# Two PSUM tiles per running sum, part of the layer norm on ScalarE, and sums of x behind the Relu, in an attention and gated MLP kernel

## Chip, cores and metric

The kernel runs on one core of a Trainium2 chip. The metric is the device time of one execution, in microseconds (us). The kernel before takes 684.58 us, the median of 3 runs (684.27 to 684.89). Its profiled execution took 684.64 us, and the span of its trace, from the first to the last instruction, is 682.9 us.

## The reference

Eight batches, 12 heads, 448 positions, 64 columns a head; d_model is 768, d_ff 1024. All data are float32.

```python
scores = scale * np.matmul(q, k.transpose(0, 1, 3, 2)) - np.log(S)
attn = 1.0 / (1.0 + np.exp(-scores))
x = np.matmul(attn, v)                      # then (B, S, 768)
h = np.maximum(x @ w_in, 0.0)
u, v = h[..., :512], h[..., 512:]
mu = np.mean(v, axis=-1, keepdims=True)
var = np.mean((v - mu) ** 2, axis=-1, keepdims=True)
v_n = (v - mu) / np.sqrt(var + 1e-06)
v_s = np.einsum('ts,bsd->btd', w_spatial, v_n) + b_spatial[None, :, None]
out = (u * v_s) @ w_out
```

So it is attention with a sigmoid, and a gated MLP whose gate is the normalised half of the hidden values, mixed over the positions.

## The kernel before

**Precision.** A float32 operand is split into a high part, rounded to the type that TensorE takes, and a low part, the remainder. A product is three matmuls: high by high, low by high, high by low (`TERMS`).

**Stages.** The loop over m = 0 to 3 takes two batches at a time, b0 = 2m and b1 = 2m + 1. Each m goes through:

1. attention: scores, sigmoid, products with the values; the result is x in two parts (`x_s`);
2. the gate stage: `gate_values` for the row tiles (0, 1), (2, 3), (4, 5) and (6,) of the 896 positions. TensorE makes the gate half of the hidden values into PSUM tile pv, 18 matmuls for a row tile and 36 for a pair. ScalarE takes the Relu into rv (L606). VectorE makes statistics (L610, L611), GpSimd the power -0.5 of the variance (L613, L614), VectorE subtracts the mean (L616, "centring"), multiplies by rstd into the high part (L628) and forms the low part (L629);
3. the spatial stage: `spatial` multiplies with w_spatial into four PSUM tiles pg, one for each batch and half of the columns; `spatial_shorts` does the eight short matmuls of the last 64 positions (L658) for all four tiles; `biased` adds the bias on VectorE (L700) and so frees a tile of pg;
4. the block stage, only for m > 0: `gated_by_blocks` makes the other half of the hidden values for both batches from seven products of blocks (a scheme with fewer products than eight). Each product is 18 matmuls, two halves of nine, one for each 128 columns. The seven add up in the PSUM tiles ua, uw and uz; between the products the running sums are copied out by ScalarE (L775) or added to sums in SBUF by VectorE (L778). `settle` applies Relu and gate, splits the result and leaves it for the output. For m = 0 `gated` does all products plainly;
5. the output: six products po of 24 matmuls, each copied out by ScalarE and stored.

The products of blocks need sums of parts of x (t2, t3, t4, t1). They are made on VectorE and ScalarE in small steps: `x_sums` is a generator of 21 steps, and `spare(n)` takes the next n of them. `gate_values` calls `spare` ahead of the Relu (8, 2, 3, 3 steps for the four groups) and once again (1 step) behind the centring. `spare(99)` behind the gate stage takes what is left. `x_last_sum` then makes t1 in place in `x_s`: three passes over 1344 columns on VectorE, a cast on ScalarE, and a last subtraction on VectorE (L582, L584, L122, L123).

**Order.** Nothing is scheduled: `in_program_order` ties each instruction to the one before on its engine, so an engine's order is that in which the code issues. Loads are issued on SP in the same way; `load_block` brings weight blocks (768 KB) into four slots as they come free.

**PSUM.** `banks(name)` takes the next of four tiles of two banks each, in turn. A tile with i = 0 and 1 holds both halves of a product, one per bank; a write to a tile waits for the readers of that tile. In the block stage `products(ps, pos, mv, begins, then)` runs the two halves, and behind each one `then(i)` copies it out or adds it.

Of the kernel before, what the change touches and what calls it, by code (L numbers as in the profile page):

```python
# [8 lines left out]
F32 = mybir.dt.float32  # L9
F32R = mybir.dt.float32r  # L10
U32 = mybir.dt.uint32
AF = mybir.ActivationFunctionType
ALU = mybir.AluOpType
# [22 lines left out]
def attn_gmlp_kernel(  # L36
# [393 lines left out]
    def spare(n):  # L430

        while jobs and n:
            if next(jobs[0], None):
                n -= 1
            else:
                jobs.pop(0)
# [150 lines left out]
    def gate_values(m, ts):  # L587

        n = len(ts)
        pv = banks(f"pv_{m}_{ts[0]}")  # L590
        for i, t in enumerate(ts):
            product(
                pv[:, i, :F],
                [
                    (
                        lambda a, cc=cc, t=t: x_s[:, a, cc, t * P : (t + 1) * P],
                        lambda c, cc=cc: w_g_s[:, cc, c, :],
                    )
                    for cc in range(NCC)
                ],  # L600
            )
        if n > 1:
            load_weights(1 if ts[0] else 5)
        spare({0: 8, 2: 2, 4: 3, 6: 3}[ts[0]])
        rv = work.tile([P, 2, 512], F32, tag="tmp", name=f"rv_{m}_{ts[0]}", bufs=3)
        nc.scalar.activation(rv[:, :n], pv[:, :n], AF.Relu)  # L606
        mv = work.tile([P, 2, 2], F32, tag="mv", name=f"mv_{m}_{ts[0]}")
        for i in range(n):
            stats = work.tile([P, 6], F32, tag="stats", name=f"stats_{m}_{ts[i]}")
            nc.vector.bn_stats(stats, rv[:, i])  # L610
            nc.vector.bn_aggr(mv[:, i], stats)  # L611
        rstd = work.tile([P, 2], F32, tag="rstd", name=f"rstd_{m}_{ts[0]}")
        nc.gpsimd.tensor_scalar_add(rstd[:, :n], mv[:, :n, 1], 1e-6)  # L613
        nc.gpsimd.tensor_tensor(rstd[:, :n], rstd[:, :n], mhalf[:, :n], op=ALU.pow)  # L614
        for i in range(n):
            nc.vector.tensor_scalar_sub(rv[:, i], rv[:, i], mv[:, i, 0:1])  # L616
        load_weights(n - 1)
        spare(1)
        for i, t in enumerate(ts):
            vn = slots["tile"][:, t]  # L620
            if t != NFULL:
                parts = [(vn[:, 0], vn[:, 1], slice(0, P))]
            else:

                a, c = slice(0, HALF), slice(HALF, P)
                parts = [(vn[a, 0], vn[c, 0], a), (vn[c, 1], vn[a, 1], c)]
            for hi, lo, rows in parts:
                nc.vector.tensor_scalar_mul(hi, rv[rows, i], rstd[rows, i : i + 1])  # L628
                nc.vector.scalar_tensor_tensor(  # L629
                    lo,  # L630
                    rv[rows, i],
                    rstd[rows, i : i + 1],
                    hi.bitcast(F32),
                    op0=ALU.mult,
                    op1=ALU.subtract,
                )
            vns[t] = vn
        if n == 1:
            load_weights(1)
# [84 lines left out]

    def settle(b, fcs, g, pu):

        nc.vector.scalar_tensor_tensor(g, pu, 0.0, g, op0=ALU.max, op1=ALU.mult)
        if b % 2:
            gs = [slots["tile"][:, fcs[0] + a, :, :S] for a in range(2)]
        elif b > 1 and not fcs[0]:  # L730
            gs = [slots["tile"][:, 4 + a, :, :S] for a in range(2)]
        else:
            gs = work.tile([P, 2, 2 * S], F32R, tag="split", name=f"gs_{b}_{fcs[0]}", bufs=3)
            gs = [gs[:, a].rearrange("p (i s) -> p i s", i=2) for a in range(2)]
        split(gs[0], gs[1], g, nc.scalar.copy)
        for i, fc in enumerate(fcs):
            hidden[b, fc] = [part[:, i] for part in gs]
        load_weights(2)

    def gated_by_blocks(m):  # L740

        b0, b1 = 2 * m, 2 * m + 1
        x = {
            name: [
                x_s[:, :, k * KH + ks, j * S : (j + 1) * S] for ks in range(KH)
            ]
            for name, k, j in (("11", 0, 0), ("21", 1, 0), ("22", 1, 1), ("t1", 0, 1))
        }
        x |= sums
        r1, r2 = (work.tile([P, 2, S], F32, tag="v", name=f"ur_{m}_{n}", bufs=2) for n in range(2))  # L750
        r3 = work.tile([P, 1024], F32, tag="raw", name=f"ur_{m}_2", bufs=4)[:, : 2 * S].rearrange(
            "p (i s) -> p i s", i=2
        )

        def products(ps, pos, mv, begins, then=None):
            w = block(pos)
            ops = [(a, ks, c) for ks in range(KH) for a, c in TERMS]
            for i in range(2):
                for n, (a, ks, c) in enumerate(ops):
                    col = (ks * 2 + i) * P  # L760
                    nc.tensor.matmul(  # L761
                        ps[:, i, :S],
                        w[:, a, col : col + P],
                        x[mv][ks][:, c],
                        start=begins and n == 0,
                        stop=n == len(ops) - 1,
                        skip_group_check=True,
                    )
                if then:
                    then(i)  # L770
            if pos + SLOTS_U < NB:
                load_block(pos + SLOTS_U)

        def copied_to(r, ps):
            return lambda i: nc.scalar.copy(r[:, i], ps[:, i, :S])  # L775

        def added_to(r, ps):
            return lambda i: nc.vector.tensor_add(r[:, i], ps[:, i, :S], r[:, i])  # L778

        pairs = (0, 1), (2, 3)  # L780
        pa = banks(f"ua_{m}")
        products(pa, 0, "11", True, copied_to(r1, pa))
        pw = banks(f"uw_{m}")
        products(pw, 1, "21", True, added_to(r1, pw))
        settle(b0, pairs[0], gates.pop((b0, pairs[0])), r1)
        products(pa, 2, "t2", False, copied_to(r2, pa))
        pz = banks(f"uz_{m}")
        products(pz, 3, "t1", True)

        def both(i):  # L790
            copied_to(r3, pa)(i)
            added_to(r3, pz)(i)

        products(pa, 4, "t3", False, both)
        settle(b1, pairs[1], gates.pop((b1, pairs[1])), r3)
        products(pa, 5, "t4", False)
        settle(b0, pairs[1], gates.pop((b0, pairs[1])), pa[:, :, :S])
        products(pz, 6, "22", False, added_to(r2, pz))
        settle(b1, pairs[0], gates.pop((b1, pairs[0])), r2)

# [259 lines left out]
    for m in range(B // 2):  # L1060
        attention(m)
        slots_of_mlp(m)
        if m:
            jobs.append(x_sums(m))
        for ts in ((0, 1), (2, 3), (4, 5), (6,)):
            gate_values(m, ts)
        if m:
            spare(99)
            x_last_sum(m)
        b0, b1 = 2 * m, 2 * m + 1  # L1070
        more = m < B // 2 - 1
        for b in (b0, b1):
            for fcs in pairs:
                spatial_room(b, fcs)
                if (b, fcs) == (b0, pairs[0]):
                    spatial(b, fcs)
        spatial_shorts(m, pairs)
        biased(b0, pairs[0])
        for b, fcs in ((b0, pairs[1]), (b1, pairs[0])):
            spatial(b, fcs)  # L1080
            biased(b, fcs)
        spatial(b1, pairs[1])
        if m:
            biased(b1, pairs[1])
            gated_by_blocks(m)
            start_loads(m + 1)
            if more:
                for pos in range(SLOTS_U):
                    load_block(pos)
            output(b0, (0, 1))  # L1090
        else:
            gated(b0, pairs[0])
            biased(b1, pairs[1])
            gated(b0, pairs[1])
            gated(b1, pairs[0])
            start_loads(m + 1)
            output(b0, (0, 1))
            gated(b1, pairs[1])
            jobs.append(weight_sums())
        spare(3)  # L1100
        output(b0, (2, 3))
        spare(3)
        output(b0, (4, 5))
        spare(3)
        if more:
            for n in range(3):
                attention_splits(*units[(m + 1) * 2 * NHP + n])
        output(b1, (0, 1))
        spare(3)
        output(b1, (2, 3))  # L1110
        spare(3)
        output(b1, (4, 5), final=not more)
        spare(8)
        if not m:
            for pos in range(SLOTS_U):
                load_block(pos)
# [55 lines left out]
```

## Time and profile before

| | |
|---|---|
| median of 3 runs | 684.58 us (684.27 to 684.89) |
| the profiled execution | 684.64 us |
| its span | 682.9 us |
| TensorE busy | 656.1 us, 96% of the span |
| VectorE busy | 416.2 us, 61% |
| ScalarE busy | 282.2 us, 41% |
| GpSimd busy | 22.6 us, 3% |
| DMA, mean over the span | 114 GB/s |

In the profile TensorE is PE (matmuls) and PEld (weight loads), VectorE is DVE, ScalarE is ACT, GpSimd is POOL and SyncE is SP. A row of the timeline has its start in us from the start of the span, its length, the engine, the line, the operation, out<-in by the program's names, the shape, and how many instructions were merged; in brackets stands how long the engine was idle before it and what released it. Matmuls are pipelined, so the distance between two starts tells more than a length.

### The profile page before, as it was taken

Reading aid. Unit: us, or ns where it says so; the run is one execution under the profiler, and the core shown is the slowest. Engines: PE = TensorE matmul, PEld = TensorE weight load, DVE = VectorE, ACT = ScalarE, POOL = GpSimd, SP = SyncE. Lnnn points to the kernel's source line nnn. Section 1 sums busy time; section 2 is a strip of 40 time slices with the busy share of each in tenths; the row PEclk is TensorE's granted clock in tenths of the full one; section 3 lists DMA queues with packets and bytes.
Section 4 is the critical chain, followed back from the end, with each engine's and each line's share of the span. In section 5 each row is a group of like instructions: output and inputs, shape, how many; then the busy total and the mean of one; then the engine's idle time right before and its main releaser. Section 6 shows DMA issues by size and latency. Waiting matters only on the chain.

```text
span 682.9 us, 10025 instructions
## 1 busy us (share of the span) xinstructions
PE 656.1 (96%) x4208; PEld 502.4 (74%) x4208; DVE 416.2 (61%) x579; ACT 282.2 (41%) x329; POOL 22.6 (3%) x63
## 2 busy tenths in 40 slices
PE   9999999999999999889999999988999999998897
PEld 3655889998666688679856678866985667886697
DVE  4989789757674598533167468843316747884310
ACT  6986313323887321121378732111137873211121
POOL 0000010000000011000000001100000000110000
PEclk9999999999999999999999999999999999999999
DMA  8754223457841000238344100024734310002112
GB/s 291 261 172 155 61 62 100 134 220 292 326 161 55 2 0 1 92 123 305 124 142 137 55 1 1 0 93 169 250 138 138 137 56 1 0 1 96 43 55 108
DMA packets 25117, 77.85 MB, mean 114 GB/s; under 512 B 2416, under 2 KB 8944, under 8 KB 25072
## 3 DMA queue, kind: packets, MB, share of 16 engines
q1 hardware_dynamic: 24784, 76.98, 32.6%
q8 instruction: 33, 0.54, 0.3%
q10 hardware_dynamic: 288, 0.23, 0.1%
q14 instruction: 12, 0.10, 0.1%
HBM read 60.69 MB, written 16.52 MB: 113 GB/s over the span
## 4 chain that ended last, share of the span: by engine, by line
PE 84%; DVE 9%; ACT 3%; POOL 1%; issue 1%; DMA 1%; SPq 0%; ACTq 0%; DVEq 0%
PE po L407 17%; PE pav L915 14%; PE psc L325 13%; PE pv L407 11%; PE ua L761 6%; PE pg L683 6%; PE pav L374 5%; PE pu L407 4%; PE uz L761 3%; PE psc L307 3%; DVE mlp L629 2%; PE uw L761 2%; DVE stats L610 1%; DVE mlp L628 1%; ACT rv L606 1%
## 5 line engine op out<-in xcount | busy, mean ns | idle before, releaser
L407 PE MATMUL pv<-w_g_s,x_s 128*128 128x512 f32 x504 | 115.4, 390 | 0.0
L407 PEld LDWEIGHTS pv<-w_g_s,x_s 128*128 128x128 f32 x504 | 94.3, 188 | 22.3 <-issue 2.1
L289 ACT ACTIVATE ats<-psc,bias_s 128x896 f32<-128x896 f32 x102 | 95.3, 1007 | 20.1 <-PE pav L915 13.7
L325 PEld LDWEIGHTS psc<-qks 64*128 64x128 f32 x840 | 77.8, 184 | 14.8 <-issue 4.9
L325 PE MATMUL psc<-qks 64*128 64x448 f32 x840 | 88.5, 364 | 0.0
L407 PE MATMUL po<-mlp,w_out_s 128*128 128x448 f32 x396 | 83.4, 364 | 0.0
L407 PEld LDWEIGHTS po<-mlp,w_out_s 128*128 128x128 f32 x396 | 75.1, 190 | 5.1
L915 PE MATMUL pav<-ats,v 64*64 64x448 f32 x720 | 76.5, 539 | 0.0
L683 PE MATMUL pg<-w_sp_s,mlp 128*128 128x448 f32 x320 | 65.8, 363 | 0.0
L683 PEld LDWEIGHTS pg<-w_sp_s,mlp 128*128 128x128 f32 x320 | 59.7, 188 | 5.4 <-issue 1.2
L915 PEld LDWEIGHTS pav<-ats,v 64*64 64x64 f32 x720 | 28.8, 132 | 37.2 <-issue 25.9
L828 ACT COPY osb<-po 128x896 f32<-128x896 f32 x23 | 20.9, 907 | 68.2 <-PE po L407 65.1
L123 DVE TENSOR_TENSOR x_s<-pav,x_s 128x896 fp32r<-128x896 f32 x16 | 17.4, 1090 | 51.1 <-ACT x_s L122 51.1
L275 DVE TENSOR_TENSOR qks<-raw,qks 128x848 fp32r<-128x848 f32 x46 | 47.3, 1038 | 1.1
L407 PE MATMUL po<-gs,w_out_s 128*128 128x448 f32 x180 | 39.2, 362 | 0.0
L407 PEld LDWEIGHTS po<-gs,w_out_s 128*128 128x128 f32 x180 | 33.8, 188 | 2.2
L268 DVE CAST qks<-raw 128x848 fp32r<-128x848 f32 x38 | 22.7, 597 | 20.5 <-PE po L407 14.8
L915 PE MATMUL pav<-at,v 64*64 64x448 f32 x216 | 32.2, 536 | 0.0
L761 PE MATMUL uz<-x_s,w_u_s 128*128 128x448 f32 x108 | 26.0, 395 | 6.0 <-DVE ur L778 6.0
L887 DVE COPY wval_s<-psc 128x896 f32<-128x896 f32 x9 | 9.8, 1090 | 35.8 <-PE psc L325 35.8
L778 DVE TENSOR_TENSOR ur<-uz,ur 128x448 f32<-128x448 f32 x12 | 7.5, 622 | 37.7 <-ACT ur L775 28.6
L761 PE MATMUL ua<-xs,w_u_s 128*128 128x448 f32 x108 | 24.3, 369 | 6.4 <-ACT ur L775 6.4
(120 smaller groups left out, 814.1 us busy)
## 6 DMA issues: line engine op xcount, KB each, us to landing
raw<-qk_dram SPq DMA_DIRECT2D x47, 456.0 KB, 5.3
w_u_s<-w_u SPq DMA_DIRECT2D x21, 768.0 KB, 5.3
v<-v_dram SPq DMA_DIRECT2D x24, 448.0 KB, 3.4
out_dram<-osb SPq DMA_DIRECT2D x23, 448.0 KB, 2.6
wraw<-w_in_dram SPq DMA_DIRECT2D x12, 512.0 KB, 4.7
wraw<-w_out_dram SPq DMA_DIRECT2D x6, 512.0 KB, 3.8
w_u<-x_s SPq DMA_DIRECT2D x4, 768.0 KB, 3.6
w_u<-w_u_s SPq DMA_DIRECT2D x3, 768.0 KB, 5.5
```

What stands on the lines that cost most here:

```text
L123: nc.vector.tensor_sub(lo, src, hi.bitcast(F32))
L268: (nc.vector.tensor_copy if b > 1 or halfway else nc.scalar.copy)(s[:, 0], raw)
L275: nc.vector.tensor_sub(s[:, 1], loaded[b, hp][:, HALF:], s[:, 0].bitcast(F32))
L289: nc.scalar.activation(at, src, AF.Sigmoid, bias=bias_s, scale=QK)
L307: nc.tensor.matmul(psc[odd * HALF : (odd + 1) * HALF, j, :S], raw[rows, :HALF], raw[rows, HALF + Q :], start=True, stop=True,)
L325: nc.tensor.matmul(psc[:, j, :S], st[rows, k : k + P], mv[rows, Q:PART], start=i == 0, stop=i == len(ops) - 1,)
L374: nc.tensor.matmul(pav[heads, odd, :S], vt[rows, t, heads], at[rows, j], start=start, stop=t == NFULL,)
L407: nc.tensor.matmul(ps, st, mv, start=i == 0, stop=i == len(ops) - 1)
L683: nc.tensor.matmul(pg[:, i, :S], st, mv, start=n == 0 and not ended, stop=n == len(ops) - 1 and ended,)
L761: nc.tensor.matmul(ps[:, i, :S], w[:, a, col : col + P], x[mv][ks][:, c], start=begins and n == 0, stop=n == len(ops) - 1, skip_group_chec ...
L828: nc.scalar.copy(osb, po[:, :, :S])
L915: ins = nc.tensor.matmul(pavs[pair][heads, i % 2, :S], vt[rows, t if t == NFULL else t + i % 2 * (NFULL + 1), heads], at[rows, j], start=i ...
```

## The change

1. In the block stage each half of a sum gets a PSUM tile of its own. `pa` is two tiles ua_0 and ua_1, of which one bank each is used. `pw` and `pz` share the tiles ub_0 and ub_1: pw in the first bank, pz in the second. `settle` takes pa as two pieces.
2. For m > 0 the centring and the high part go from VectorE to ScalarE, as Identity with the negated mean as bias and with rstd as scale. VectorE negates the mean; the low part stays on VectorE.
3. The `spare` calls are placed otherwise: 8 steps ahead of the first Relu only, then 2 steps behind the statistics in each group, and the rest behind the gate stage. `x_last_sum` comes behind the first `biased`.

```diff
-        spare({0: 8, 2: 2, 4: 3, 6: 3}[ts[0]])
+        if not ts[0]:
+            spare(8)
         rv = work.tile([P, 2, 512], F32, tag="tmp", name=f"rv_{m}_{ts[0]}", bufs=3)
         nc.scalar.activation(rv[:, :n], pv[:, :n], AF.Relu)
...
+        mean = work.tile([P, 2], F32, tag="mean", name=f"mean_{m}_{ts[0]}")
         nc.gpsimd.tensor_scalar_add(rstd[:, :n], mv[:, :n, 1], 1e-6)
         nc.gpsimd.tensor_tensor(rstd[:, :n], rstd[:, :n], mhalf[:, :n], op=ALU.pow)
+        if m:
+            nc.vector.tensor_scalar_mul(mean[:, :n], mv[:, :n, 0], -1.0)
+            spare(2)
         for i in range(n):
-            nc.vector.tensor_scalar_sub(rv[:, i], rv[:, i], mv[:, i, 0:1])
+            if m:
+                nc.scalar.activation(rv[:, i], rv[:, i], AF.Identity, bias=mean[:, i : i + 1])
+            else:
+                nc.vector.tensor_scalar_sub(rv[:, i], rv[:, i], mv[:, i, 0:1])
         load_weights(n - 1)
-        spare(1)
...
-                nc.vector.tensor_scalar_mul(hi, rv[rows, i], rstd[rows, i : i + 1])
+                if m:
+                    nc.scalar.activation(
+                        hi, rv[rows, i], AF.Identity, scale=rstd[rows, i : i + 1]
+                    )
+                else:
+                    nc.vector.tensor_scalar_mul(hi, rv[rows, i], rstd[rows, i : i + 1])
...
     def settle(b, fcs, g, pu):
-        nc.vector.scalar_tensor_tensor(g, pu, 0.0, g, op0=ALU.max, op1=ALU.mult)
+        for at, by in pu if isinstance(pu, list) else [(g, pu)]:
+            nc.vector.scalar_tensor_tensor(at, by, 0.0, at, op0=ALU.max, op1=ALU.mult)
...
-                        ps[:, i, :S],
+                        ps[i],
...
-        pa = banks(f"ua_{m}")
+        pa = [banks(f"ua_{m}_{i}")[:, 0, :S] for i in range(2)]
         products(pa, 0, "11", True, copied_to(r1, pa))
-        pw = banks(f"uw_{m}")
+        both = [banks(f"ub_{m}_{i}") for i in range(2)]
+        pw, pz = ([ps[:, n, :S] for ps in both] for n in range(2))
         products(pw, 1, "21", True, added_to(r1, pw))
         settle(b0, pairs[0], gates.pop((b0, pairs[0])), r1)
         products(pa, 2, "t2", False, copied_to(r2, pa))
-        pz = banks(f"uz_{m}")
         products(pz, 3, "t1", True)
...
         products(pa, 5, "t4", False)
-        settle(b0, pairs[1], gates.pop((b0, pairs[1])), pa[:, :, :S])
+        g = gates.pop((b0, pairs[1]))
+        settle(b0, pairs[1], g, [(g[:, i], pa[i]) for i in range(2)])
...
         if m:
             spare(99)
-            x_last_sum(m)
...
         spatial_shorts(m, pairs)
         biased(b0, pairs[0])
+        if m:
+            x_last_sum(m)
```

The changed kernel's lines from here on are later by 1 to 15, so L606 becomes L607, L761 becomes L774, L700 becomes L712.

**ScalarE, end of the gate stage of m = 1.** pv_4 and pv_6 are the PSUM tiles of the row tiles (4, 5) and (6,), rv their Relu, xt and xs sums of x, mlp the parts of the normalised values. Before:

```order
L554 CAST xs_1_2088<-xt_1_2094 128x448
L606 ACTIVATE rv_4_2227<-pv_4_2186 128x1024
L561 CAST xs_1_2088<-xt_1_2094 128x448
L606 ACTIVATE rv_6_2269<-pv_6_2246 128x512
L570 CAST x_1_2_2092<-xt_1_2094 128x448
```

And now:

```order
L607 ACTIVATE rv_4_2231<-pv_4_2194 128x1024
L554 CAST xs_1_2092<-xt_1_2098 128x448
L622 ACTIVATE rv_4_2231<-rv_4_2231,mean_4_2241 128x512 x2
L636 ACTIVATE mlp_2053<-rv_4_2231,rstd_4_2240 128x512 x2
L607 ACTIVATE rv_6_2273<-pv_6_2254 128x512
L622 ACTIVATE rv_6_2273<-rv_6_2273,mean_6_2280 128x512
L636 ACTIVATE mlp_2053<-rv_6_2273,rstd_6_2279 128x512
L561 CAST xs_1_2092<-xt_1_2098 128x448
L570 CAST x_1_2_2096<-xt_1_2098 128x448
```

Six Identities have come in ahead of the last two casts; each Relu stands ahead of the cast that it followed, and the Relu of pv_6 follows the Identities of the group (4, 5).

**VectorE, from the last step of the sums of x to the bias sums of m = 1.** The lines L582 to L123 are `x_last_sum`, L700 and L712 `biased`. Before:

```order
L574 TENSOR_TENSOR x_1_2_2092<-xt_1_2094,x_1_2_2092 128x448
L582 TENSOR_TENSOR wval_s<-x_s 128x1344
L584 TENSOR_TENSOR wval_s<-wval_s,x_s 128x1344 x2
L123 TENSOR_TENSOR x_s<-wval_s,x_s 128x3x448
L700 TENSOR_TENSOR g_0_2321<-pg_0_2289,b_bc 128x2x448
L700 TENSOR_TENSOR g_2_2343<-pg_2_2310,b_bc 128x2x448
L700 TENSOR_TENSOR g_0_2365<-pg_0_2311,b_bc 128x2x448
L700 TENSOR_TENSOR wval_s<-pg_2_2312,b_bc 128x896
```

And now:

```order
L574 TENSOR_TENSOR x_1_2_2096<-xt_1_2098,x_1_2_2096 128x448
L712 TENSOR_TENSOR g_0_2328<-pg_0_2296,b_bc 128x2x448
L582 TENSOR_TENSOR wval_s<-x_s 128x1344
L584 TENSOR_TENSOR wval_s<-wval_s,x_s 128x1344 x2
L123 TENSOR_TENSOR x_s<-wval_s,x_s 128x3x448
L712 TENSOR_TENSOR g_2_2355<-pg_2_2317,b_bc 128x2x448
L712 TENSOR_TENSOR g_0_2377<-pg_0_2318,b_bc 128x2x448
L712 TENSOR_TENSOR wval_s<-pg_2_2319,b_bc 128x896
```

The first bias sum is ahead of `x_last_sum`; the other three stay behind it.

**TensorE, start of the block stage of m = 1.** w_u_s holds the weight blocks, and the number at the end of a name tells one PSUM tile from another. Before:

```order
L683 MATMUL pg_2_2312<-w_sp_s,mlp_2049 128x448 x20
L761 MATMUL ua_2391<-x_s,w_u_s 128x448 x18
L761 MATMUL uw_2413<-x_s,w_u_s 128x448 x18
L761 MATMUL ua_2391<-xs_0_2087,w_u_s 128x448 x6
L761 MATMUL ua_2391<-xs_1_2088,w_u_s 128x448 x3
L761 MATMUL ua_2391<-xs_0_2087,w_u_s 128x448 x6
L761 MATMUL ua_2391<-xs_1_2088,w_u_s 128x448 x3
L761 MATMUL uz_2459<-x_s,w_u_s 128x448 x18
```

And now:

```order
L695 MATMUL pg_2_2319<-w_sp_s,mlp_2053 128x448 x20
L774 MATMUL ua_0_2403<-x_s,w_u_s 128x448 x9
L774 MATMUL ua_1_2404<-x_s,w_u_s 128x448 x9
L774 MATMUL ub_0_2426<-x_s,w_u_s 128x448 x9
L774 MATMUL ub_1_2427<-x_s,w_u_s 128x448 x9
L774 MATMUL ua_0_2403<-xs_0_2091,w_u_s 128x448 x6
L774 MATMUL ua_0_2403<-xs_1_2092,w_u_s 128x448 x3
L774 MATMUL ua_1_2404<-xs_0_2091,w_u_s 128x448 x6
L774 MATMUL ua_1_2404<-xs_1_2092,w_u_s 128x448 x3
```

The matmuls stand in the same order; a tile that took 18 in a row is now two tiles that take nine each.

## Rows read from the trace of the kernel before

**Rows 1.** The page, its first view: busy us (share of the span) x instructions.
```profile
PE 656.1 (96%) x4208; PEld 502.4 (74%) x4208; DVE 416.2 (61%) x579; ACT 282.2 (41%) x329; POOL 22.6 (3%) x63
```

**Rows 2.** Waits: engine, line waited for: us in total, times, longest.
```profile
PE ua L761 <- ACT ur L775: 10.1, 12, 1.5
...
PE pg L658 <- ACT rv L606: 3.0, 3, 1.0
```

**Rows 3.** Timeline of m = 1, block stage: start, us, instruction, count [idle before <- releaser].
```profile
276.31 2.07 PE L761 MATMUL ua<-x_s,w_u_s 128*128 128x448 f32 x9
...
279.00 2.08 PE L761 MATMUL ua<-x_s,w_u_s 128*128 128x448 f32 x9 [0.62 <-ACT ur L775]
...
290.98 3.76 PE L761 MATMUL uz<-x_s,w_u_s 128*128 128x448 f32 x18
...
294.58 1.97 PE L761 MATMUL ua<-xs,w_u_s 128*128 128x448 f32 x9
...
307.56 2.08 PE L761 MATMUL uz<-x_s,w_u_s 128*128 128x448 f32 x9 [2.01 <-DVE ur L778]
...
309.48 1.36 PE L407 MATMUL po<-mlp,w_out_s 128*128 128x448 f32 x6
```

**Rows 4.** Timeline of TensorE in the block stage of m = 2.
```profile
445.25 2.08 PE L761 MATMUL ua<-x_s,w_u_s 128*128 128x448 f32 x9
...
476.51 3.56 PE L761 MATMUL uz<-x_s,w_u_s 128*128 128x448 f32 x9 [2.01 <-DVE ur L778]
479.87 1.49 PE L407 MATMUL po<-mlp,w_out_s 128*128 128x448 f32 x6
```

**Rows 5.** One us of that stage: us, busy by engine, PEclk (clock), DMA share, GB/s.
```profile
477.00:478.00 1.00, 1.00 (x4) 0.88 (x3) 0.00 (x0) 0.00 (x0) 0.00 (x0) 0.50 1.00 401
```

**Rows 6.** Timeline around the short matmuls, m = 0 (first two rows) and m = 1.
```profile
98.83 1.12 PE L658 MATMUL pg<-w_sp_s,mlp 64*128 64x448 f32 x8
99.88 4.47 PE L683 MATMUL pg<-w_sp_s,mlp 128*128 128x448 f32 x21
...
261.51 0.87 PE L658 MATMUL pg<-w_sp_s,mlp 64*128 64x448 f32 x5
...
262.74 0.59 ACT L606 ACTIVATE rv<-pv 128x512 f32<-128x512 f32 x1
...
263.99 12.27 PE L683 MATMUL pg<-w_sp_s,mlp 128*128 128x448 f32 x60
```

**Rows 7.** Groups by form, 228 to 311: readers of the sums; count | busy, mean ns | idle.
```profile
L775 ACT COPY ur<-ua 128x448 f32<-128x448 f32 x6 | 3.2, 532 | 16.1 <-PE ua L761 16.1
...
L778 DVE TENSOR_TENSOR ur<-uz,ur 128x448 f32<-128x448 f32 x4 | 2.5, 622 | 11.7 <-ACT ur L775 9.5 <-PE uz L761 2.2
```

**Rows 8.** Durations (ns min/median/max; by form: mean) of like operations on ScalarE and VectorE.
```profile
L289 ACT ACTIVATE ats<-ats,bias_s x22: 1031/1033/1061, 11.9 to 559.5; 128x896 f32<-128x896 f32 x22
...
L122 ACT CAST mlp<-g x8: 937/940/943, 138.2 to 651.8; 128x896 fp32r<-128x896 f32 x8
...
L570 ACT CAST x<-xt 128x448 fp32r<-128x448 f32 x3 | 1.6, 567 | 5.7 <-DVE xt L567 5.7
...
L616 DVE TENSOR_SCALAR rv<-rv,mv 128x512 f32<-128x512 f32 x7 | 3.0, 470 | 0.0
...
L610 DVE BATCH_NORM_STATS2 stats<-rv 128x6 f32<-128x512 f32 x7 | 4.7, 678 | 1.2 <-ACT rv L606 1.2
```

**Rows 9.** Timeline of the gate stage of m = 1, where the walk starts and ends.
```profile
228.71 27.50 PE L407 MATMUL pv<-w_g_s,x_s 128*128 128x512 f32 x120
...
245.42 1.03 ACT L606 ACTIVATE rv<-pv 128x1024 f32<-128x1024 f32 x1 [1.60 <-PE pv L407]
...
265.01 0.80 POOL L614 TENSOR_TENSOR rstd<-rstd,mhalf 128x1 f32<-128x1 f32 x1
...
267.57 1.55 DVE L582 TENSOR_TENSOR wval_s<-x_s 128x1344 f32<-128x1344 f32 x1
...
275.17 3.08 DVE L700 TENSOR_TENSOR g<-pg,b_bc 128x896 f32<-128x896 f32 x3
```

More of the change, by code (lines that the diff above doesn't have):

```diff
@@ L774, in copied_to @@
         def copied_to(r, ps):
-            return lambda i: nc.scalar.copy(r[:, i], ps[:, i, :S])
+            return lambda i: nc.scalar.copy(r[:, i], ps[i])
         def added_to(r, ps):
-            return lambda i: nc.vector.tensor_add(r[:, i], ps[:, i, :S], r[:, i])
+            return lambda i: nc.vector.tensor_add(r[:, i], ps[i], r[:, i])
         pairs = (0, 1), (2, 3)
-        pa = banks(f"ua_{m}")
+        pa = [banks(f"ua_{m}_{i}")[:, 0, :S] for i in range(2)]
         products(pa, 0, "11", True, copied_to(r1, pa))
-        pw = banks(f"uw_{m}")
+        both = [banks(f"ub_{m}_{i}") for i in range(2)]
+        pw, pz = ([ps[:, n, :S] for ps in both] for n in range(2))
         products(pw, 1, "21", True, added_to(r1, pw))
@@ L786, in gated_by_blocks, with copied_and_added @@
         products(pa, 2, "t2", False, copied_to(r2, pa))
-        pz = banks(f"uz_{m}")
         products(pz, 3, "t1", True)
-        def both(i):
+        def copied_and_added(i):
             copied_to(r3, pa)(i)
             added_to(r3, pz)(i)
-        products(pa, 4, "t3", False, both)
+        products(pa, 4, "t3", False, copied_and_added)
         settle(b1, pairs[1], gates.pop((b1, pairs[1])), r3)
         products(pa, 5, "t4", False)
-        settle(b0, pairs[1], gates.pop((b0, pairs[1])), pa[:, :, :S])
+        g = gates.pop((b0, pairs[1]))
+        settle(b0, pairs[1], g, [(g[:, i], pa[i]) for i in range(2)])
         products(pz, 6, "22", False, added_to(r2, pz))
```

## The prediction

> **What bounds the kernel now.** I read the busy shares of the page first: TensorE is busy for 96% of the span [rows 1], so only a place where it stands still can be worth time. The list of waits comes next. It names, among those that the diff touches, ua behind ScalarE's copies (12 times, four for each of m = 1, 2, 3) and pg behind ScalarE's Relu (once for each) [rows 2].
>
> Then the timeline of the block stage (`gated_by_blocks`) of m = 1, to see how these waits arise [rows 3]. A product of 18 matmuls runs without a break from 290.98 to 294.58: 3.60 us, or 1.80 for one half of nine. But the first half of ua starts at 276.31 and the second at 279.00, 2.69 later: it waited for the copy of the first half, which lies in another bank of the same tile. The last half of uz waits 2.01 for VectorE in the same way. The stage lasts from 276.31 to 309.48, 33.17 us, for 14 halves that need 14 x 1.80 = 25.20: **7.97 us lost**.
>
> The stage of m = 2 runs from 445.25 to 479.87, 34.62 us, 1.45 more. This is the clock: its last nine matmuls take 3.36 (476.51 to 479.87) where m = 1 needs 1.92 [rows 3, 4]. From 477 to 478 the granted clock was 0.50, the lower of the two levels (1.2 and 2.4 GHz); what went before was TensorE's idle time of 2.01 us [rows 4, 5]. The stage of m = 3 repeats this; m = 1, with the same idle time, does not. So it is **1.44 us in two of three stages**.
>
> Ahead of this stage lie two more losses. The eight short matmuls of pg take 98.83 to 99.88, 1.05 us, in m = 0, but 261.51 to 263.99, 2.48, in m = 1: they need the PSUM of pv_6, whose Relu starts only at 262.74, behind a cast of x sums on ScalarE. That is **1.43 lost**. The 60 matmuls behind them need 60 x 0.20 = 12.00, but ua starts 12.32 after them, as VectorE's first bias sum starts at 275.17: **0.32 lost** [rows 3, 6, 9].
>
> **The change part by part.**
>
> *Two tiles per sum.* Now each half waits for the reader of its own tile. Between two uses of a tile lies at least the other half (1.80 us). By the first half of ua, a reader needs 2.69 - 1.80 = 0.89 behind the last matmul, 0.53 of it the copy; a sum on VectorE is 0.62 [rows 3, 7]. So in the closest place (t3, then t4) the reader is done 0.9 ahead of need. The settling passes on VectorE and ScalarE stand between these readers; laid out one by one, the last of b0's hidden values is there 1 us ahead of the po matmul that reads it. So I take all of 7.97: **-7.97**. VectorE's gating product over pa becomes two; nothing waits for it in that stretch, so it costs nothing, and 0.15 if it did. Four tiles in place of three fill the pool of four: ua_1 now takes the place of pg's second tile, ub_0 of the third, ub_1 of the fourth, and the first po that of ua_0, read 2 us earlier. The loads of weight blocks and of the next m on SP are issued behind the same products, in the same order, and move forward with them.
>
> *Sums of x behind the Relu.* The Relu of pv_6 no longer queues behind the cast that waits for VectorE. By the walk below it ends at 261.3 (before: 262.74 + 0.59), and the matmul that needs it comes later, at about 262: **-1.43**. With the first bias sum ahead of the last sum of x, ua_0's tile is free early: **-0.32**.
>
> *Centring and high part on ScalarE.* Per m VectorE gives up seven centrings at 0.47 and eight high parts of the same width, some 7 us [rows 8]. It gains four negations of 128 x 2, between nothing and 0.47; so few elements are nearer to nothing, I take 0.1. But now VectorE waits for ScalarE. What is an Identity with a scale or bias per partition worth on 128 x 512? On ScalarE, SBUF to SBUF, 896 columns take 0.94 as a cast and 1.03 as a Sigmoid with such a bias: 0.09 for the operand. A cast of 448 takes 0.567, so a column is 0.83 ns, 512 of them 0.62, and with the operand **0.71** [rows 8]. Lower bound 0.59, the Relu of 512 [rows 6]; upper bound 1.03, the Relu of 1024 [rows 9]; I take 0.71, being put together from the nearest rows. In a queue each starts 0.1 before the former ends, as I read it, so a step of 0.62.
>
> A rule of the Trainium skill speaks against this part: its page "ScalarE: Activation LUTs", section "Rules for kernel authors", puts adds and multiplies on VectorE, not on ScalarE. For the single operation the rows agree, 0.47 against 0.71. By the rows, with these passes left on VectorE and the first bias sum ahead, the second bias sum would end at 277.3 in place of the 278.7 below, and the sum would be 4.2 us lower, 658.7.
>
> The walk of m = 1 [rows 6 to 9]. The Relu of pv_2 starts when TensorE is through with it, at 245.42. The pv matmuls take 27.5 / 120 = 0.229 each, so pv_4 is ready 36 of them (8.2) later: its Relu runs from 253.6 to 254.6. Statistics of two tiles 1.7 (0.68 for a pass, and the aggregation), negation 0.1: 256.4. Two x sums at 0.62 and their hand-over: 257.7. ScalarE's cast follows, then two centrings and two high parts, starting at 258.2, 258.85, 259.45, 260.1; then the Relu of pv_6 from 260.7 to 261.3. VectorE's low parts (some 0.7 each, from the sums of 448 by width) end at 261.65; statistics of pv_6 and the negation 262.55; two x sums 263.7. GpSimd's power takes 0.80, 1.5 with the addition ahead of it and the hand-overs, so the high part starts at 264.0 and the low part ends at 265.5. Four x sums, a cast on ScalarE and the last low part of t4: 269.1. First bias sum, 1.0: 270.1. The last sum of x takes 7.60 (267.57 to 275.17 before): 277.7. **The second bias sum ends at 278.7.**
>
> TensorE comes earlier: 261.51 + 1.05 + 12.00 + 1.80 = 276.36 for the second half of the first product. It waits for pg's second tile until 278.7: **+2.36**, and 0.12 for the restart (1.92 for a half behind a wait, 1.80 else). Behind it ub_0 is due at 280.6 with its tile free at 279.7, ub_1 at 282.4 against 280.8: no further wait. Bounds: six moved passes lie on the chain, so 1.65 at 0.59 each, 4.3 at 1.03; and 0 if VectorE's share of the walk is 2.4 too long.
>
> *Clock.* The new wait is an idle time of about 2.2 us after dense work, much like the one behind which the clock fell in two of three stages. I take two falls again; they cancel against those of before.
>
> **Sum.** Per m 7.97 + 1.43 + 0.32 - 2.48 = 7.24; times three 21.7; clock 0. The profiled execution took 684.64 (span 682.9), the median of the three runs is 684.58, next to it. 684.6 - 21.7 = **662.9 us**.
>
> **The rivals.**
> - *VectorE comes in time*: no new wait, no fall of the clock: 662.9 - 3 x 2.48 - 2 x 1.44 = 652.6. For it: 7 us less work per m on VectorE. Against: four groups of tiles now need two more hand-overs each, and the x sums that filled VectorE's waits are used up or put off. Chance 0.17.
> - *The change does not do what it says*: uw and uz share the tiles ub, and a half could again be held by a reader of the other sum. If the last uz kept its wait (2.01 and 0.12), it is 3 x 2.13 = 6.4 more: 669.3. Against: by the order, the other sum's reader stands at least one product back. Chance 0.06.
> - *Slower*: ScalarE sets the end of the gate stage. The wait at ua_1 would have to grow from 2.36 to 9.6 (7.97 + 1.43 + 0.32 - 0.12), 7.2 more on six passes, 1.2 each: it decides from 1.9 us for an Identity. At 2.2 us it would be 684.6 + 3 x 1.7 = 690. Against: 1.03 for twice the columns [rows 9]. Chance 0.04.
>
> **How the numbers follow.** The forecast has 0.73. Its own range goes from 658 (wait 1.65, no fall: 662.9 - 2.1 - 2.9) to 668.7 (wait 4.3: 662.9 + 5.8). Of the first rival, values between 654 and 658 (a wait of well under 1 us) are as likely as none at all. So the range is 654 to 669, leaving out some 0.15. A measurement can tell 0.2% (1.4 us) from no change; only the last rival is near or above 684: faster 0.95, same 0.01, slower 0.04.
>
> **What would show it.** In the profile after: no wait of TensorE between halves behind the first, 1.80 a half; no wait of pg for the Relu; one wait of ua_1 for VectorE's bias sum of about 2.2 us in each m; Identities of 0.71. If ua_1 does not wait, the walk of VectorE is wrong and the time falls under 657. If the clock falls nowhere, no falls cancel and it is 660. If halves still wait for copies, the tile was not what held them.

## The result, and the profile after

The changed kernel takes **663.68 us** (median of 4 runs, 663.2 to 664.51) against 684.55 before on the same chips: the ratio is 0.9696, 95% interval 0.968 to 0.9713. The forecast was 662.9, the range 654 to 669. The span of the profiled execution went from 682.9 to 661.5.

The first view of the page after, busy us (share of the span) x instructions, as in [rows 1]:

```profile
PE 649.5 (98%) x4208; PEld 503.5 (76%) x4208; DVE 398.7 (60%) x549; ACT 311.1 (47%) x374; POOL 27.8 (4%) x63
```

TensorE has the same 4208 matmuls and 98% of the span in place of 96%. ScalarE gained 29 us of work, VectorE lost 17.5.

TensorE's waits in the list of waits after, to be put beside [rows 2]:

```profile
PE ua L774 <- DVE g L712: 7.2, 3, 2.4
PE warm L416 <- DVE ats L412: 1.2, 1, 1.2
```

Before, the list also had these two rows for VectorE's sums between the products:

```profile
PE uz L761 <- DVE ur L778: 6.0, 3, 2.0
PE uw L761 <- DVE ur L778: 2.4, 3, 0.8
```

The waits for ScalarE's copies, for VectorE's sums and for the Relu are gone. One new wait stands in their place: ua for VectorE's bias sum, once for each m, 2.4 us. (The second row, at the start of the kernel, was there before.)

The timeline of TensorE after, m = 1, from the short matmuls to the first po, beside [rows 3, 6] (dots stand for rows left out, of TensorE or of other engines):

```profile
261.32 1.09 PE L670 MATMUL pg<-w_sp_s,mlp 64*128 64x448 f32 x8
...
262.34 12.28 PE L695 MATMUL pg<-w_sp_s,mlp 128*128 128x448 f32 x60
...
274.45 1.97 PE L774 MATMUL ua<-x_s,w_u_s 128*128 128x448 f32 x9
...
278.81 3.18 PE L774 MATMUL ua<-x_s,w_u_s 128*128 128x448 f32 x9 [2.39 <-DVE g L712]
...
281.79 4.30 PE L774 MATMUL ub<-x_s,w_u_s 128*128 128x448 f32 x18
...
285.92 3.76 PE L774 MATMUL ua<-xs,w_u_s 128*128 128x448 f32 x18
...
289.52 3.76 PE L774 MATMUL ub<-x_s,w_u_s 128*128 128x448 f32 x18
...
303.92 1.36 PE L407 MATMUL po<-mlp,w_out_s 128*128 128x448 f32 x6
```

The eight short matmuls now take 261.32 to 262.34, 1.02 us, where they took 2.48. The first half of ua starts at 274.45; the second could start 1.80 later, but starts at 278.81, after 2.39 us of idle time. From 285.92 on each product of 18 matmuls takes 3.60. From the shorts to po it is 42.60 us, where it was 47.97.

In between, the matmuls are slow: the second half of ua and the two halves of ub take 7.11 (278.81 to 285.92) where 1.92 + 3.60 = 5.52 would do. One us at a time (us, busy PE, PEld, DVE, ACT, POOL, granted clock, DMA share, GB/s), as in [rows 5]:

```profile
278.00:279.00 1.00, 0.19 (x1) 0.20 (x2) 1.00 (x2) 0.00 (x0) 0.00 (x0) 1.00 0.00 0
280.00:281.00 1.00, 1.00 (x4) 0.91 (x3) 0.75 (x1) 0.00 (x0) 0.00 (x0) 0.50 0.00 0
283.00:284.00 1.00, 1.00 (x7) 0.93 (x6) 0.00 (x0) 0.00 (x0) 0.00 (x0) 1.00 0.81 203
```

While TensorE was idle the granted clock was still 1.00; in the matmuls that follow it is 0.50, the lower level, and then 1.00 again: 1.59 us lost. The stage of m = 2 shows the same, that of m = 3 does not:

```profile
601.08 1.97 PE L774 MATMUL ua<-x_s,w_u_s 128*128 128x448 f32 x9
...
605.44 2.08 PE L774 MATMUL ua<-x_s,w_u_s 128*128 128x448 f32 x9 [2.40 <-DVE g L712]
607.36 3.76 PE L774 MATMUL ub<-x_s,w_u_s 128*128 128x448 f32 x18
...
610.96 3.76 PE L774 MATMUL ua<-xs,w_u_s 128*128 128x448 f32 x18
```

There the half behind the wait takes 1.92 (605.44 to 607.36) and the rest runs at 1.80 a half.

### The profile page after: what moved, and what is told of

Read it like the earlier page. It is cut to its first block, busy times and chain, and to the rows that moved or that the text cites. A ratio compares the mean times of both kernels' runs of the same rounds, so it can differ in the third digit from the quotient of the medians.

```text
span 661.5 us, 10047 instructions
## 1 busy us (share of the span) xinstructions
PE 649.5 (98%) x4208; PEld 503.5 (76%) x4208; DVE 398.7 (60%) x549; ACT 311.1 (47%) x374; POOL 27.8 (4%) x63
## 4 chain that ended last, share of the span: by engine, by line
PE 88%; DVE 8%; ACT 3%; issue 1%; POOL 1%; POOLq 0%
PE po L407 17%; PE pv L407 16%; PE pav L929 15%; PE psc L325 14%; PE ua L774 6%; PE ub L774 5%; PE pav L374 5%; PE pu L407 4%; PE psc L307 3%; PE pg L695 2%; DVE wval_s L584 1%; DVE mlp L641 1%; DVE g L712 1%; DVE stats L611 1%; DVE x_s L123 1%; DVE wval_s L582 1%
## 5 line engine op out<-in xcount | busy, mean ns | idle before, releaser
L123 DVE TENSOR_TENSOR x_s<-pav,x_s 128x896 fp32r<-128x896 f32 x16 | 17.4, 1090 | 50.8 <-ACT x_s L122 50.8
L641 DVE SCALAR_TENSOR_TENSOR mlp<-rv,rstd,mlp 128x512 fp32r<-128x512 f32 (+1 forms) x32 | 23.5, 750 | 22.2 <-ACT mlp L636 21.7
L774 PE MATMUL ub<-x_s,w_u_s 128*128 128x448 f32 x162 | 35.4, 373 | 0.0
L774 PEld LDWEIGHTS ub<-x_s,w_u_s 128*128 128x128 f32 x162 | 32.0, 197 | 2.4
```

Of the source, the lines that this page charges most:

```text
L123: nc.vector.tensor_sub(lo, src, hi.bitcast(F32))
L641: nc.vector.scalar_tensor_tensor(lo, rv[rows, i], rstd[rows, i : i + 1], hi.bitcast(F32), op0=ALU.mult, op1=ALU.subtract,)
L774: nc.tensor.matmul(ps[i], w[:, a, col : col + P], x[mv][ks][:, c], start=begins and n == 0, stop=n == len(ops) - 1, skip_group_check=True,)
```

## The experiments

The theory behind the prediction has three parts: the split by itself removes the waits between the halves; the new wait comes from where the last sum of x stands in VectorE's order; and the passes that moved to ScalarE make that wait longer rather than shorter. The rival is that the moved passes carry the gain, by relieving VectorE. A separate question is whether the fall of the clock belongs to the idle time.

### The split alone

The kernel before with the change of `settle` and `gated_by_blocks`, and nothing else:

```diff
-        pa = banks(f"ua_{m}")
+        pa = [banks(f"ua_{m}_{i}")[:, 0, :S] for i in range(2)]
...
+        both = [banks(f"ub_{m}_{i}") for i in range(2)]
+        pw, pz = ([ps[:, n, :S] for ps in both] for n in range(2))
```

> The kernel before with the two tiles per sum alone. My theory: all of the stage's loss goes (3 x 7.97) and the clock's falls at its end with it (3.1), and no new wait comes, because VectorE's bias sums follow each other as before: 684.6 - 23.9 - 3.1 = 657.6, faster than the whole change (663.7). The wait of pg for the Relu stays, 1.0 us idle for each m. Rival: the split needs VectorE to be relieved, since its sums between the products come late; then new waits of ub for VectorE appear in the block stage and the time is above 664.

Measured: 657.96 us, ratio 0.9615 (0.9601 to 0.9629). Its waits and its block stage of m = 1:

```profile
PE pg L658 <- ACT rv L606: 3.0, 3, 1.0
```

```profile
276.63 3.88 PE L762 MATMUL ua<-x_s,w_u_s 128*128 128x448 f32 x18
...
280.35 3.76 PE L762 MATMUL ub<-x_s,w_u_s 128*128 128x448 f32 x18
...
301.95 1.36 PE L407 MATMUL po<-mlp,w_out_s 128*128 128x448 f32 x6
```

The stage takes 276.63 to 301.95, 25.32 us in place of 33.17 [rows 3]. No wait is left in it, and no stage has a fall of the clock. So **the split alone is worth 26.4 us, more than the whole change**: the other two parts together cost 5.7.

### Everything but the split

The changed kernel with `settle` and `gated_by_blocks` of before.

> The changed kernel with the old PSUM tiles in the block stage; the new placing of the x sums and the passes on ScalarE stay. My theory: what is left of the gain is the wait of the short matmuls (1.43) and the start of ua (0.32), for each m: 684.6 - 5.3 = 679.3; the waits between the halves are back. Rival: the moved passes carry a good part of the gain; then under 675.

Measured: 679.4 us, ratio 0.9924 (0.9907 to 0.9941). The waits between the halves are back in full [rows 2]:

```profile
PE ua L773 <- ACT ur L787: 10.1, 12, 1.5
PE uz L773 <- DVE ur L790: 6.0, 3, 2.0
PE uw L773 <- DVE ur L790: 2.4, 3, 0.8
```

What is left of the gain is about 5 us, as forecast for the Relu of pv_6 and the start of ua. The wait at ua_1 does not show here, since the old tile ua needs only the first bias sum; the second half waits for a copy anyway.

### Centring and high part back on VectorE

The changed kernel without the negated mean, with the passes of before; the places of the `spare` calls stay:

```diff
-            nc.vector.tensor_scalar_mul(mean[:, :n], mv[:, :n, 0], -1.0)
             spare(2)
         for i in range(n):
-            if m:
-                nc.scalar.activation(rv[:, i], rv[:, i], AF.Identity, bias=mean[:, i : i + 1])
-            else:
-                nc.vector.tensor_scalar_sub(rv[:, i], rv[:, i], mv[:, i, 0:1])
+            nc.vector.tensor_scalar_sub(rv[:, i], rv[:, i], mv[:, i, 0:1])
...
-                if m:
-                    nc.scalar.activation(
-                        hi, rv[rows, i], AF.Identity, scale=rstd[rows, i : i + 1]
-                    )
-                else:
-                    nc.vector.tensor_scalar_mul(hi, rv[rows, i], rstd[rows, i : i + 1])
+                nc.vector.tensor_scalar_mul(hi, rv[rows, i], rstd[rows, i : i + 1])
```

> The changed kernel with centring and high part back on VectorE (no negated mean), all else kept. My theory: ScalarE's passes lengthen the chain to the second bias sum; without them the wait at ua_1 falls from 2.4 to about 1.5 us idle, under what the clock was seen to fall behind: 663.7 - 3 x 0.95 - 3.2 = 657.6; between 655 and 661. Rival: VectorE needs the relief of 7 us for each m; then the second bias sum comes later, the wait at ua_1 is longer than 2.4 and the time above 664.

Measured: 656.94 us, ratio 0.9602 (0.9588 to 0.9616). TensorE around the wait, and the second and third bias sums on VectorE, m = 1:

```profile
274.71 1.97 PE L764 MATMUL ua<-x_s,w_u_s 128*128 128x448 f32 x9
...
277.86 2.08 PE L764 MATMUL ua<-x_s,w_u_s 128*128 128x448 f32 x9 [1.19 <-DVE g L702]
279.78 3.76 PE L764 MATMUL ub<-x_s,w_u_s 128*128 128x448 f32 x18
```

```profile
276.72 2.08 DVE L702 TENSOR_TENSOR g<-pg,b_bc 128x896 f32<-128x896 f32 x2
```

The idle time at ua_1 is 1.19 in place of 2.39, and the half behind it runs at full clock. Three times 1.2 us less waiting and two falls of the clock fewer (3.2) are 6.8; the kernel is 6.7 us faster than the changed one. So the move to ScalarE is a loss here, though it frees VectorE of some 17.5 us of work (the page's busy time: 398.7 after, 416.2 in this run).

This kernel is also the one with the split alone plus the new places of the sums of x, so the 5.7 come apart: the new places gain 1.0 (657.96 to 656.94), the passes on ScalarE cost 6.7.

### Work in the place of the wait

The changed kernel with 12 matmuls ahead of the second half of ua, into a bank that nobody reads:

```diff
+                if pos == 0 and i == 0:
+                    for _ in range(12):
+                        nc.tensor.matmul(
+                            idle[:, 1, :S], w[:, 0, :P], x[mv][0][:, 0], start=True, stop=True
+                        )
...
+        pas = [banks(f"ua_{m}_{i}") for i in range(2)]
+        pa = [ps[:, 0, :S] for ps in pas]
+        idle = pas[0]
```

> The changed kernel with 12 more matmuls (2.4 us) into the unused bank of ua_0, run in the place of the wait at ua_1; their result is read by nobody. They change the idle time only. If the clock falls because of that idle time, it no longer falls: 663.7 - 3.2 = 660.5, and the halves behind run at 1.80 in all three stages. If the fall has another cause, the time stays at 663 to 664.5 and two stages still show a stretch at the lower level.

Measured: 660.21 us, ratio 0.965 (0.9634 to 0.9666). The stage of m = 2, in which the changed kernel had a fall (the x12 are the added matmuls):

```profile
436.34 1.97 PE L774 MATMUL ua<-x_s,w_u_s 128*128 128x448 f32 x9
438.14 2.56 PE L784 MATMUL ua<-x_s,w_u_s 128*128 128x448 f32 x12
440.70 2.08 PE L774 MATMUL ua<-x_s,w_u_s 128*128 128x448 f32 x9
442.62 3.76 PE L774 MATMUL ub<-x_s,w_u_s 128*128 128x448 f32 x18
446.22 3.76 PE L774 MATMUL ua<-xs,w_u_s 128*128 128x448 f32 x18
```

Each product behind runs at 3.60, in all three stages. The second half starts as late as before, 4.36 behind the first (436.34 to 440.70), for it waits for the same bias sum; only TensorE is not idle until then. So 3.5 us of the changed kernel's time (two falls of 1.6 in its trace are 3.2) are the clock's answer to the idle time, not the wait itself. The prediction had said 660 for a kernel without a fall.

### Four places for the last sum of x

The changed kernel puts `x_last_sum` behind the first of four bias sums. Three kernels put it elsewhere. The first puts it ahead of all four, where it was before:

```diff
             spare(99)
+            x_last_sum(m)
...
         biased(b0, pairs[0])
-        if m:
-            x_last_sum(m)
```

> The changed kernel with the last sum of x back ahead of all bias sums. If VectorE's order at this place sets the wait, then ua_0 waits for the first bias sum, about 3.3 us idle, and ua_1 not at all: 663.7 + 3 x 0.9 = 666.4, up to 668 if the clock falls in all three stages. Rival (the wait at ua_1 hangs on ScalarE's queue, not on this order): no change, 663 to 664.5.

Measured: 665.79 us, ratio 0.9747 (0.9717 to 0.9777). The list of waits, the stage of m = 1 and that of m = 2:

```profile
PE ua L774 <- DVE g L712: 9.5, 3, 3.2
```

```profile
277.91 3.88 PE L774 MATMUL ua<-x_s,w_u_s 128*128 128x448 f32 x18 [3.18 <-DVE g L712]
281.63 3.76 PE L774 MATMUL ub<-x_s,w_u_s 128*128 128x448 f32 x18
```

```profile
440.43 5.27 PE L774 MATMUL ua<-x_s,w_u_s 128*128 128x448 f32 x18 [3.18 <-DVE g L712]
445.54 3.76 PE L774 MATMUL ub<-x_s,w_u_s 128*128 128x448 f32 x18
```

Now ua_0 waits 3.18 for the first bias sum and ua_1 does not wait. The order of VectorE is what sets the wait. The clock falls again in two of three stages: ua's 18 matmuls take 3.72 at m = 1 and 5.11 at m = 2, with the same idle time; at m = 3 they take 5.09. Of its four executions three took 665.27 to 666.21 and one 669.47, at the lowest mean granted clock of the four (0.989); of that one there is no timeline.

The second puts it behind the third bias sum:

```diff
         biased(b0, pairs[0])
-        if m:
-            x_last_sum(m)
         for b, fcs in ((b0, pairs[1]), (b1, pairs[0])):
             spatial(b, fcs)
             biased(b, fcs)
+        if m:
+            x_last_sum(m)
```

> The changed kernel with the last sum of x behind the third bias sum. My theory: ua_0, ua_1 and ub_0 find their tiles free, and only ub_1 waits for the fourth bias sum, under 1 us; no fall of the clock: 663.7 - 3.2 - 3 x 1.55 = 655.9. Rival: the last sum of x is needed sooner than that, and the wait moves to the product of t1 (fourth product); then above 660.

Measured: 656.12 us, ratio 0.9593 (0.9575 to 0.961). The one wait that is left is that of ub_1 for the fourth bias sum, as expected:

```profile
PE ub L774 <- DVE wval_s L712: 2.9, 3, 1.0
```

The third puts it behind all four. The fourth bias sum's result then needs the place where the last sum of x was made, so that goes to a tile of the pool "v" and the rest of `wval_s`, in two pieces:

```diff
+        pair = work.tile([P, 2, S], F32, tag="v", name=f"xl_{m}", bufs=2)
+        for ks, t in ((slice(0, 2), pair), (slice(2, KH), spare_words)):
...
         biased(b0, pairs[0])
-        if m:
-            x_last_sum(m)
...
             biased(b1, pairs[1])
+            x_last_sum(m)
             gated_by_blocks(m)
```

> The changed kernel with the last sum of x behind all four bias sums, in two pieces (two blocks in a tile of the v pool, one in wval's free words, since the fourth bias sum fills the rest). My theory: no wait at all is left in the block stage: 663.7 - 3.2 - 3 x 2.5 = 653.0. Rival: the sums of the second product stand behind it on VectorE and are late, so ub's t1 halves wait; then 655 or more, with a wait of ub for VectorE.

Measured: **653.47 us**, ratio 0.9555 (0.9539 to 0.957). Of TensorE's matmuls only the one at the start of the kernel is still in the list of waits. The timeline of VectorE at m = 1, below it, shows where the time for the last sum of x was:

```profile
PE warm L416 <- DVE ats L412: 1.2, 1, 1.2
```

```profile
269.38 3.08 DVE L717 TENSOR_TENSOR g<-pg,b_bc 128x896 f32<-128x896 f32 x3
...
274.95 1.09 DVE L717 TENSOR_TENSOR wval_s<-pg,b_bc 128x896 f32<-128x896 f32 x1 [2.50 <-PE pg L700]
275.96 1.08 DVE L584 TENSOR_TENSOR xl<-x_s 128x896 f32<-128x896 f32 x1
...
282.07 0.62 DVE L590 TENSOR_TENSOR x_s<-wval_s,x_s 128x448 fp32r<-128x448 f32 x1
```

Three bias sums run one after another from 269.38; then VectorE is idle for 2.50 until the spatial products end, adds the fourth, and makes the last sum of x by 282.7, while TensorE works on the first two products. It is needed for the fourth, which starts at 285.95.

One small wait is left, which the list books on the weight loads (PEld), three times:

```profile
PEld ua L779 <- ACT ur L793: 1.5, 3, 0.5
```

```profile
278.36 3.76 PE L779 MATMUL ub<-x_s,w_u_s 128*128 128x448 f32 x18
...
281.19 0.57 ACT L587 CAST x_s<-wval_s 128x448 fp32r<-128x448 f32 x1 [0.91 <-DVE wval_s L586]
281.66 0.96 ACT L793 COPY ur<-ua 128x448 f32<-128x448 f32 x2
...
282.24 3.88 PE L779 MATMUL ua<-xs,w_u_s 128*128 128x448 f32 x18
```

The copy of ua_0 now stands behind the casts of the last sum of x on ScalarE, so the third product starts 3.88 behind the second in place of 3.60. That is 0.28 for each m, 0.8 us in all: the expected "no wait at all" did not quite come.

The last kernel of this kind has the passes back on VectorE as well:

> The kernel t1_last with centring and high part back on VectorE. My theory: once the last sum of x is out of the way, nothing that TensorE waits for hangs on those passes, so it is within 1 us of t1_last. Rival: VectorE's relief is worth something by itself; then it is over 2 us slower than t1_last.

Measured: 653.53 us, ratio 0.9557 (0.9542 to 0.9573), which can't be told from 653.47. With the last sum of x out of the way, it makes no difference that can be measured which engine has the passes.

## Why the prediction was right

**The waits between the halves (-7.97 for each m): right.** The split alone shows the stage at 25.32 where 25.20 was forecast.

**The Relu of pv_6 (-1.43) and the start of ua (-0.32): the first right, the second a little too large.** The shorts lost their wait (-1.46), and ua_0 starts 12.11 behind the start of the 60 matmuls in place of 12.32. That is 0.21, not 0.32: the sum had put the 60 matmuls at 12.00. But as long as VectorE's bias sums come later than TensorE, this only makes TensorE arrive earlier at the next wait. In the kernel with the passes on VectorE, which has the split and this part, the gain over the split alone is about 1 us, hardly more than the runs scatter, not 5.

**The walk of VectorE (+2.36 for each m): right.** Walked: the Relu of pv_4 at 253.6, centring from 258.2, the Relu of pv_6 at 260.7, the high part of pv_6 at 264.0, the last sum of x from 270.1, the second bias sum done at 278.7. The timeline after has:

```profile
253.34 1.03 ACT L607 ACTIVATE rv<-pv 128x1024 f32<-128x1024 f32 x1 [1.53 <-PE pv L407]
...
258.00 1.33 ACT L622 ACTIVATE rv<-rv,mean 128x512 f32<-128x512 f32 x2
...
260.46 0.58 ACT L607 ACTIVATE rv<-pv 128x512 f32<-128x512 f32 x1
...
263.94 0.72 ACT L636 ACTIVATE mlp<-rv,rstd 128x512 fp32r<-128x512 f32 x1 [0.72 <-POOL rstd L616]
...
270.07 1.55 DVE L582 TENSOR_TENSOR wval_s<-x_s 128x1344 f32<-128x1344 f32 x1
...
277.67 2.08 DVE L712 TENSOR_TENSOR g<-pg,b_bc 128x896 f32<-128x896 f32 x2
```

The second bias sum ends 1.0 to 1.1 behind 277.67, at 278.7. The idle time is 2.39 where about 2.2 was forecast, and the second half starts 2.56 late (278.81 - 274.45 - 1.80) where the sum had 2.36. The Identity was put together as 0.71 from a cast, a Sigmoid and a column's price [rows 8]:

```profile
L622 ACT ACTIVATE rv<-rv,mean x21: 706/718/726, 243.0 to 589.1; 128x512 f32<-128x512 f32 x21
```

With rstd as scale it took 0.71 at the median as well. The negation of the mean, for which I took 0.1 between bounds of nothing and 0.47, measured 0.17.

**The clock (0): right in number, and in part by luck.** Two of three stages had a fall, now m = 1 and 2 in place of 2 and 3, at 1.59 in place of 1.44 each. That the idle time brings the falls was right: with it filled with work, no stage has one. That there would again be two was a guess from one execution, and executions of one kernel differ in this (last section).

**The sum.** It was 21.7 us; the spans differ by 21.4, the medians by 20.9. By stages, from the shorts to po: m = 1 saved 5.37, m = 2 6.80 (430.47 to 479.87 before, 424.63 to 467.23 after), m = 3 8.07 (600.73 to 649.81 before, 587.95 to 628.96 after). They differ by the falls alone: 1.59 after at m = 1, 1.44 before and 1.60 after at m = 2, and 1.11 before at m = 3, as far as that one lies ahead of po. Without them each stage saved 6.96, where 7.24 was forecast: 0.20 of the difference is the longer wait, 0.11 the start of ua, less 0.03 at the shorts. That makes 20.9 for the three stages. So the spans come as near as 21.4 because some 0.7 us were saved elsewhere, which the sum did not have.

**The rivals.** VectorE did not come in time; the kernel with the last sum of x at the end shows that 653.5 would then have been reached, where 652.6 was said; the 0.28 for each m that is left there is about the difference. The tile ub, shared by two sums, held nobody back: the list of waits after has no row for it. For the slower rival an Identity would have had to take 1.9 us; it took 0.71.

**The rule against the change.** The prediction set the Trainium skill, page "ScalarE: Activation LUTs", section "Rules for kernel authors", against this part: adds and multiplies belong on VectorE. By the runs it would have been right to follow it here: the same kernel with these passes on VectorE takes 656.94. I had put that variant at 658.7. Its second bias sum came later than I said (277.8 against 277.3, wait 1.19 against 0.9), which alone would have made it slower than 658.7; and I had left out that a shorter wait also spares the two falls of the clock, some 3 us, which outweighs that.

## What to carry to other kernels

A tile that holds two halves of a product makes the second half wait for the reader of the first, though they lie in different banks: where the tiles of the pool allow it, give each half its own. An engine that is 60% busy can still set the time by its order: look for the long step (here 7.6 us) that stands ahead of short ones which free what the busiest engine waits for, and put it where its result is just early enough. Moving work to an idler engine adds hand-overs to the chain. Here it cost 6.7 us where that chain ended in a wait of the busiest engine, and gained nothing where it did not (653.47 against 653.53).

## What the runs showed of the hardware that was not expected

Behind idle times of TensorE of about 2.0 to 3.2 us the granted clock fell to 0.50 in some stages and not in others of the same execution, with the same work ahead: 2.01 before, two of three; 2.39 after, two of three; 3.18 with the last sum of x first, two of three. In that last kernel it was the first stage that had no fall, with 3.18 us idle. So between these lengths it is not the length alone that decides. Nor is it the stage: before, behind 2.01 us, the falls were at m = 2 and 3; in the kernel with everything but the split, behind the same 2.01 or 2.02 us, they were at m = 1 and 2.

Executions of one kernel differ too. Of seven of the kernel before, on one chip, three had spans of 681.3 to 681.4 us at a mean granted clock of 0.997, four 682.6 to 683.3 at 0.994 or 0.995. That is about what one fall costs; but these executions have no timeline, so that it is a fall is not shown. What decides was not tried. Behind 0.98, 1.19 or, before, 1.51 us no stage had a fall. A fall cost about 1.4 to 1.6 us each time.
